# Phase rows and masks of small matrices moved from VectorE to GpSimd, and two weight loads joined

## The chip, the cores and the metric

The kernel runs on one core of one Trainium2 chip. The metric is the device time of one execution in microseconds (us); the median of several runs is compared. Beside the times there is one execution taken with a hardware profiler, from which all rows below come. The engines are named as in the profile: PE (matrix multiply), PEld (its weight loads), DVE (VectorE), ACT (ScalarE), POOL (GpSimd) and SP (SyncE, which here only issues DMAs).

## The reference

The input is one sequence of 2048 rows of 640 features in bfloat16. It is normalised, goes through a gated long convolution and through a dense two-layer network, and both results are joined:

```python
xn = _layernorm(x)                                  # x = A_q, 1 x 2048 x 640
k_shift = sum over t of k_pad[:, t:t+S, :] * shift_k[:, ks-1-t]      # ks = 4
kv = k_shift * v
y = irfft(rfft(kv padded to 2S) * rfft(ssm_k padded to 2S))[:S]      # float32, then bf16
s = xn * (y + kv * ssm_D)
g = silu(gelu(xn @ w1 + b1) @ w2 + b2)              # w1 640 x 1728, w2 1728 x 640
return x + s * g
```

## The kernel before

Partition p holds the 16 rows 16p to 16p+15 of the sequence. The 16 rows are worked in four chunks of four (`CH = 4`), so a chunk is 512 rows: it is normalised, transposed by PE into `xnT`, multiplied with w1 in 14 blocks of 128 columns (`ffn1`, L467, and `first_block`, L786, for the first six blocks of the first chunk), put through gelu by ACT into `hT`, and multiplied with w2 (L500).

The convolution is done as a Fourier transform of length 8192 in two factors. The first factor's matrices `WA` and `WB` are sines of integer phases: `prod` holds the phases (built at L304, cut to 13 bits by `f1_phase` at L308), and ACT takes the sines (`f1_sines`). The second factor uses three small 128x128 matrices `mats`, each made of 32x32 blocks on the diagonal. They too come from phases: `small_iotas` writes rows of column numbers with POOL (L340), `small_bits` takes bits of the partition number on DVE (a bitwise and at L350 and a cast at L352, for the masks 30, 1 and 96), `small_first` makes two scalars of them (L362, L363), `small_second` builds three phase rows `ph` (L356 twice, L371), `small_phase` finishes them, builds three masks (L377 to L381) and cuts the phases to five bits in `q` (L384, L385), ACT takes the sine (`small_sine`, L390), and DVE multiplies with the masks (`small_mats`, L394).

The order on each engine is written out by hand: first the function `prologue`, then a long list of steps, `PLAN`, each a short name that a table maps to a function. Each engine runs its own instructions in that order and waits only for what an instruction needs. So an engine that has little to do runs far ahead of the place in the program that the text suggests. In `PLAN`, `s` is `small_phase`, `w` is `f1_phase`, `X1` the load of the second chunk of x, `ls4` to `ls7` the second chunk's statistics (L421, L422), `lv1` its variance plus epsilon (L426), `lr1` the power to the -1/2 on POOL (L430), `lb1` the bias (L434), `ln4.d` to `ln7.a` its normalisation on DVE (L444) or ACT (L442), `tt` transposes on PE (L451), `cv` a step of the four-tap convolution on DVE (L590, L594, L583), `ss` and `sm` the sine and the product of the small matrices.

In `prologue` the first chunk is done by hand, in two halves of two rows: `bn` and `ag` are statistics (L748, L751), `sq` and `rc` the reciprocal root (L754 on ACT, L757 on DVE), `norm_dve` the normalisation (L760), `turn` the transposes on PE (L777), `turned_out` the copies back (L148 on DVE, L147 on ACT), and `first_block` the products with w1.

The loads are issued by SP (L239 for x, L266 for w1, L244 to L246 for k, L273 to L276 for w2, L269 for the filter, L249 for v), with four small ones on ACT's queue. Each load counts on one of eight semaphores in turn, and waits until the load eight places before it, on the same semaphore, has landed.

Of the kernel before, what the change touches and what calls it, by code (L numbers as in the profile page):

```python
# [15 lines left out]
ALU = mybir.AluOpType  # L16
# [4 lines left out]
F = 1728  # L21
# [11 lines left out]
TURNS = "231221331312001123202202330111320201303303312100"  # L33

PLAN = """
em6 he0 he1 s w X1 em7 em5 he2 K1 em4 ls6 ls7 ls4 ls5 K0 h11 he5 ee5.a ee4.a h8 h6 he4 ee7.a he3 he8 B1 h13 B2 B0 cv16
lv1 cv8 cv17 cv9 he6 lr1 lb1 C4 he13 ee6.a cv18 cv19 cv10 ln4.d h10 he11 he10 h7 he7 h12 h9 ln5.a he12 ln7.a ln6.d cv0
cv20 tt9 tt7 C1 C3 C0 he9 C2 cv11 cv1 te7.d cv21 ws0 tt6 tt8 te8.d g1 tt5 te9.d ss sm cv12 cv2 cv3 te5.d K3 X2 V5 K2
V4 V0 V3 V6 g0 ws1 ws2 ge0 ge1 g2 ge2 d kt1 kt7 kt6 kc7.a kt3 kt0 cv22 cv4 te6.d kc6.d kt2 kt9 kc3.d kc2.d kc0.a V2 X3
V7 kc9.d kc1.a kt12 kt4 kf2 kf23 kt11 kf8 ke2.d kc12.a V1 kt13 kc4.d kc13.d kf0 ke23.a ke8.a gm0.d kf6 kf22 ke6.a  # L40
# [51 lines left out]
def kernel(  # L92
# [15 lines left out]
    nc = tc.nc  # L108
# [127 lines left out]
    def load_x(c):  # L236
        for h in range(1 if c else 2):
            js = slice(2 * h, CH if c else 2 * h + 2)
            nc.sync.dma_start(out=xn_tiles[c][:, js, :], in_=x_v[:, c * CH:(c + 1) * CH, :][:, js, :])  # L239
# [22 lines left out]
                nc.scalar.dma_start(out=prm[FT:FT + DT, :], in_=A_ssm_D.rearrange("(t p) -> t p", p=P))  # L262

    def load_w1(i):
        a, b = ((0, 384), (384, 768), (768, F))[i]
        nc.sync.dma_start(out=w1_sb[:, :, a:b], in_=B_w1.rearrange("(t p) f -> p t f", p=P)[:, :, a:b])  # L266

    def load_kf(t):
# [63 lines left out]
    sm = {}  # L332
# [19 lines left out]
            nc.vector.tensor_copy(out=f, in_=i)  # L352
            sm.setdefault("in", []).append(f)

    def stt(o, a, s, b, op0, op1):
        nc.vector.scalar_tensor_tensor(out=o, in0=a, scalar=s, in1=b, op0=op0, op1=op1)  # L356

    def small_first():
        n_in, c_in, r_in = sm["in"]
        n_out, c_out, r_out = sm["cols"]  # L360
        sm.update(ph=scratch([3, P], F32), mask=scratch([3, P], F32), c8=scratch([1], F32), c16=scratch([1], F32))
        nc.vector.tensor_single_scalar(out=sm["c8"], in_=c_in, scalar=8.0, op=ALU.mult)  # L362
        nc.vector.tensor_single_scalar(out=sm["c16"], in_=c_in, scalar=16.0, op=ALU.mult)  # L363

    def small_second():
        n_in, c_in, r_in = sm["in"]
        n_out, c_out, r_out = sm["cols"]
        ph = sm["ph"]
        stt(ph[:, 0, :], n_out, n_in[:, 0:1], c_out, ALU.mult, ALU.add)
        stt(ph[:, 2, :], n_out, n_in[:, 0:1], c_out, ALU.mult, ALU.subtract)  # L370
        nc.vector.tensor_scalar(out=ph[:, 1, :], in0=ph[:, 2, :], scalar1=sm["c16"][:, 0:1], scalar2=None, op0=ALU.add)  # L371

    def small_phase():
        n_in, c_in, r_in = sm["in"]
        n_out, c_out, r_out = sm["cols"]
        ph, mask = sm["ph"], sm["mask"]
        nc.vector.tensor_scalar(out=ph[:, 2, :], in0=ph[:, 2, :], scalar1=8.0, scalar2=None, op0=ALU.add)  # L377
        nc.vector.tensor_scalar(out=ph[:, 0, :], in0=ph[:, 0, :], scalar1=sm["c8"][:, 0:1], scalar2=None, op0=ALU.subtract)
        nc.vector.tensor_scalar(out=mask[:, 0, :], in0=r_out, scalar1=r_in[:, 0:1], scalar2=None, op0=ALU.is_equal)
        for i in (1, 2):  # L380
            nc.vector.tensor_scalar(out=mask[:, i, :], in0=r_out, scalar1=r_in[:, 0:1], scalar2=2.0 / 4096.0,  # L381
                                    op0=ALU.is_equal, op1=ALU.mult)
        q = scratch([3, P], I32)
        nc.vector.tensor_single_scalar(out=q, in_=ph, scalar=float(8 + 16 + 128), op=ALU.add)  # L384
        nc.vector.tensor_single_scalar(out=q, in_=q, scalar=31, op=ALU.bitwise_and)  # L385
        sm.update(q=q, sn=scratch([3, P], F32))

# [352 lines left out]
    def prologue():  # L740
# [48 lines left out]
        make_identity(nc, ident[:])  # L789
        nc.vector.memset(prm[:], 0.0)  # L790
        load_x(0)
        for i in range(3):
# [118 lines left out]
```

## Time and profile before

| | before |
|---|---|
| median of 3 runs | 198.41 us (198.15 to 198.58) |
| the profiled execution's own time | 198.26 us |
| its span, first to last instruction | 196.5 us |
| PE busy | 186.5 us (95%) |
| DVE busy | 175.3 us (89%) |
| ACT busy | 162.6 us (83%) |
| POOL busy | 42.9 us (22%) |
| granted TensorE clock | 0.998 |

A row of the order of time gives the start in us, the time in us, the engine, the source line, the operation, what it writes and reads, the size, how many instructions are merged in the row, and in brackets the idle time before it with what ended it. A row of the table of waits gives who waited for whom, the total in us, how often, and the longest. A row of a table by stretch gives for each engine the busy time and, as (x), the instructions; then the clock, the DMA engines' share and GB/s.

### The profile page before, as it was taken

The numbers are of one execution on the slowest core, as the hardware profiler recorded it, in microseconds if no ns is written. First come the engines' busy times: TensorE is split into PE (matmuls) and PEld (weight loads), VectorE is DVE, ScalarE is ACT, GpSimd is POOL, SyncE is SP. The second block draws the span as 40 slices with busy tenths as digits, with TensorE's granted clock in tenths as the row PEclk, the third lists the DMA queues.
The fourth block names the chain that finished last, engine by engine and source line by source line (L and its number), as shares of the span: only waits on it lengthen the run. The fifth ranks groups of instructions, "written<-read, shape, count | busy, mean of one in ns | idle before, by whom it ended". The sixth has DMA issues, their size and how long they took to land.

```text
span 196.5 us, 5128 instructions
## 1 busy us (share of the span) xinstructions
PE 186.5 (95%) x1927; PEld 111.1 (57%) x1939; DVE 175.3 (89%) x379; ACT 162.6 (83%) x323; POOL 42.9 (22%) x76
## 2 busy tenths in 40 slices
PE   7899969999999999998999999999999999999991
PEld 2585447787665445663566443465665544657771
DVE  7989999999999999989999999999999920489992
ACT  3577999999999999999998999999679758991030
POOL 8100300004454032344030000000475500002220
PEclk9999999999999999999999999999999999999999
DMA  6999999974888899798788999596969659994344
GB/s 200 374 378 345 342 408 414 393 294 153 319 326 337 268 325 368 303 341 341 267 274 312 287 338 329 158 303 228 272 243 336 223 188 350 397 398 157 145 173 137
DMA packets 27057, 57.69 MB, mean 294 GB/s; under 512 B 3032, under 2 KB 15513, under 8 KB 27032
## 3 DMA queue, kind: packets, MB, share of 16 engines
q1 hardware_dynamic: 22528, 39.65, 57.6%
q0 software_dynamic: 4320, 17.70, 24.3%
q8 instruction: 15, 0.25, 0.5%
q14 instruction: 10, 0.08, 0.2%
q10 hardware_dynamic: 184, 0.01, 0.1%
HBM read 33.76 MB, written 18.35 MB: 265 GB/s over the span
## 4 chain that ended last, share of the span: by engine, by line
PE 59%; ACT 14%; DMA 12%; DVE 9%; issue 3%; SPq 1%; DVEq 0%
PE banks L500 20%; PE banks L467 19%; ACT area L147 7%; PE banks L414 7%; DMA area<-in_A_k_dram 5%; DMA area<-in_A_ssm_k_dram 5%; PE banks L550 5%; DVE area L590 3%; DMA w_sb<-in_B_w_dram 2%; ACT hT L479 2%; DVE area L594 2%; PE banks L719 2%; PE banks L720 2%; DVE area L148 2%; PE banks L451 1%
## 5 line engine op out<-in xcount | busy, mean ns | idle before, releaser
L147 ACT CAST area<-banks 128x426 bf16<-128x426 f32 (+2 forms) x175 | 80.7, 614 | 4.2 <-PE banks L414 3.4
L500 PE MATMUL banks<-w_sb,hT 128*128 128x320 bf16 (+1 forms) x462 | 65.8, 295 | 0.4 <-ACT sl L508 0.3
L500 PEld LDWEIGHTS <-hT 128*128 128x128 bf16 x462 | 43.5, 98 | 18.9 <-issue 3.7
L467 PE MATMUL banks<-xnT,w_sb 128*128 128x512 bf16 x218 | 52.8, 379 | 0.7
L674 DVE TENSOR_TENSOR area<-banks,area 128x426 bf16<-128x426 f32 (+1 forms) x96 | 50.1, 591 | 0.2
L479 ACT ACTIVATE hT<-banks,b_f 128x512 bf16<-128x512 f32 x52 | 35.4, 718 | 4.9 <-PE banks L467 3.0
L467 PEld LDWEIGHTS <-w_sb 128*128 128x128 bf16 x230 | 21.5, 97 | 25.7 <-issue 3.7
L508 ACT ACTIVATE sl<-banks 128x320 bf16<-128x320 f32 (+1 forms) x33 | 14.8, 476 | 14.2 <-PE banks L500 12.9
L594 DVE TENSOR_TENSOR area<-area 128x1280 bf16<-128x1280 bf16 x32 | 25.4, 816 | 0.3
L414 PE MATMUL banks<-area,mats 32*32 32x426 bf16 (+1 forms) x768 | 20.7, 345 | 0.5 <-DVE area L148 0.2
L728 DVE TENSOR_TENSOR area<-banks,xn 128x426 bf16<-128x426 f32 (+1 forms) x18 | 9.9, 591 | 12.3 <-ACT hT L479 10.2
L704 POOL DMA_DIRECT2D scrC<-area x16 | 11.7, 730 | 42.1 <-ACT area L147 40.0
L590 DVE TENSOR_TENSOR area<-area 128x1280 bf16<-128x1280 bf16 x24 | 19.1, 812 | 0.0
L550 PE MATMUL banks<-area,WA 128*128 128x212 bf16 (+1 forms) x64 | 15.6, 299 | 0.1
L550 PE MATMUL banks<-area,WB 128*128 128x214 bf16 (+1 forms) x64 | 15.5, 299 | 0.0
L565 POOL DMA_DIRECT2D scrK<-area x16 | 8.8, 553 | 29.3 <-ACT area L147 28.9
L414 PEld LDWEIGHTS <-mats 32*32 32x32 bf16 x768 | 8.1, 88 | 12.4 <-issue 10.3
L148 DVE CAST area<-banks 128x426 bf16<-128x426 f32 (+1 forms) x21 | 11.4, 593 | 1.6 <-PE banks L414 0.8
L576 POOL DMA_DIRECT2D scrU<-area x16 | 8.6, 543 | 14.5 <-ACT area L147 13.7
L430 POOL TENSOR_TENSOR rs<-ve,mhalf 128x4 f32<-128x4 f32 x3 | 4.0, 1350 | 31.0 <-DVE ve L426 31.0
L421 DVE BATCH_NORM_STATS2 st<-xn 128x6 f32<-128x320 bf16 x24 | 10.3, 472 | 0.0
L515 DVE TENSOR_TENSOR xn<-xn,sl 128x320 bf16<-128x320 bf16 (+1 forms) x33 | 9.8, 307 | 0.2 <-ACT sl L508 0.2
(106 smaller groups left out, 195.8 us busy)
## 6 DMA issues: line engine op xcount, KB each, us to landing
scrK<-area POOLq DMA_DIRECT2D x16, 320.0 KB, 3.2
scrU<-area POOLq DMA_DIRECT2D x16, 320.0 KB, 3.7
area<-scrK SPq DMA_DIRECT2D x16, 320.0 KB, 6.6
area<-area SPq DMA_DIRECT2D x32, 160.0 KB, 3.8
area<-scrU SPq DMA_DIRECT2D x16, 320.0 KB, 4.8
scrC<-area POOLq DMA_DIRECT2D x16, 320.0 KB, 4.2
area<-scrC SPq DMA_DIRECT2D x16, 320.0 KB, 6.5
area<-in_A_k_dram SPq DMA_DIRECT2D x4, 640.0 KB, 10.0
```

Source lines behind the costliest of these rows:

```text
L147: return nc.scalar.copy(out=out_ap, in_=in_ap)
L148: return nc.vector.tensor_copy(out=out_ap, in_=in_ap)
L414: nc.tensor.matmul(out=out[b, :], lhsT=mats[a, m, a], rhs=rhs[a, :], start=start, stop=stop)
L467: nc.tensor.matmul(out=ps, lhsT=w1_sb[:, t, ft * P:(ft + 1) * P], rhs=xnT[:, t, :], start=(t == 0), stop=(t == DT - 1))
L479: nc.scalar.activation(out=hT[:, ft, :], in_=one(("h", i)), func=ACT.Gelu_apprx_tanh, bias=b1_f[:, ft:ft + 1], scale=1.0)
L500: nc.tensor.matmul(out=ps[:, 0:ws.stop - ws.start], lhsT=hT[0:M, ft, q * P:(q + 1) * P], rhs=w2_sb[0:M, ft, hs.start + ws.start:hs.start + ...
L508: nc.scalar.activation(out=sl[:, ws], in_=one(key)[:, 0:ws.stop - ws.start], func=ACT.Silu)
L550: nc.tensor.matmul(out=ps[:, dst], lhsT=(WA, WB)[r][:, n2, :], rhs=rows[:, n2 % 2, src], start=True, stop=True)
L590: nc.vector.tensor_tensor(out=uc, in0=uc, in1=tmp, op=ALU.add)
L594: nc.vector.tensor_tensor(out=tmp if s else uc, in0=kh[:, r0:r0 + KC, :], in1=w_exp[:, j:j + 1, :].to_broadcast([P, KC, D]), op=ALU.mult)
L674: nc.vector.tensor_tensor(out=flat(("p", i))[:, x * w:x * w + w], in0=one(("mu", i))[:, 0:w], in1=flat(key)[:, cols(j)], op=ALU.mult)
L704: nc.gpsimd.dma_start(out=pair_view(scrC)[g2], in_=pair(("c", g2)))
```

## The change

Three things are changed.

The three phase rows, their two additions and the three masks are built by POOL instead of DVE. The two instructions that DVE did with two operands and a scalar (L356) become one product and two additions of two operands, so POOL has nine instructions for DVE's eight. They are all in `small_second` now.

The two bit steps that stay on DVE (`small_phase`) move in `PLAN` from in front of `w` to behind `lv1`.

The first two loads of w1, columns 0 to 383 and 384 to 767, become one. Eight loads then come before the second chunk's x instead of nine.

```diff
 PLAN = """
-em6 he0 he1 s w X1 em7 em5 he2 K1 em4 ls6 ls7 ls4 ls5 K0 h11 he5 ee5.a ee4.a h8 h6 he4 ee7.a he3 he8 B1 h13 B2 B0 cv16
-lv1 cv8 cv17 cv9 he6 lr1 lb1 C4 he13 ee6.a cv18 cv19 cv10 ln4.d h10 he11 he10 h7 he7 h12 h9 ln5.a he12 ln7.a ln6.d cv0
+em6 he0 he1 w X1 em7 em5 he2 K1 em4 ls6 ls7 ls4 ls5 K0 h11 he5 ee5.a ee4.a h8 h6 he4 ee7.a he3 he8 B1 h13 B2 B0 cv16
+lv1 s cv8 cv17 cv9 he6 lr1 lb1 C4 he13 ee6.a cv18 cv19 cv10 ln4.d h10 he11 he10 h7 he7 h12 h9 ln5.a he12 ln7.a ln6.d
...
     def load_w1(i):
-        a, b = ((0, 384), (384, 768), (768, F))[i]
+        a, b = ((0, 768), (768, F))[i]
...
     def small_second():
...
-        stt(ph[:, 0, :], n_out, n_in[:, 0:1], c_out, ALU.mult, ALU.add)
-        stt(ph[:, 2, :], n_out, n_in[:, 0:1], c_out, ALU.mult, ALU.subtract)
-        nc.vector.tensor_scalar(out=ph[:, 1, :], in0=ph[:, 2, :], scalar1=sm["c16"][:, 0:1], scalar2=None, op0=ALU.add)
+        nc.gpsimd.tensor_scalar(out=ph[:, 1, :], in0=n_out, scalar1=n_in[:, 0:1], scalar2=None, op0=ALU.mult)
+        nc.gpsimd.tensor_tensor(out=ph[:, 0, :], in0=ph[:, 1, :], in1=c_out, op=ALU.add)
+        nc.gpsimd.tensor_tensor(out=ph[:, 2, :], in0=ph[:, 1, :], in1=c_out, op=ALU.subtract)
+        nc.gpsimd.tensor_scalar(out=ph[:, 1, :], in0=ph[:, 2, :], scalar1=sm["c16"][:, 0:1], scalar2=None, op0=ALU.add)
+
+        mask = sm["mask"]
+        nc.gpsimd.tensor_scalar(out=ph[:, 2, :], in0=ph[:, 2, :], scalar1=8.0, scalar2=None, op0=ALU.add)
+        nc.gpsimd.tensor_scalar(out=ph[:, 0, :], in0=ph[:, 0, :], scalar1=sm["c8"][:, 0:1], scalar2=None, op0=ALU.subtract)
+        nc.gpsimd.tensor_scalar(out=mask[:, 0, :], in0=r_out, scalar1=r_in[:, 0:1], scalar2=None, op0=ALU.is_equal)
+        for i in (1, 2):
+            nc.gpsimd.tensor_scalar(out=mask[:, i, :], in0=r_out, scalar1=r_in[:, 0:1], scalar2=2.0 / 4096.0,
+                                    op0=ALU.is_equal, op1=ALU.mult)

     def small_phase():
-        nc.vector.tensor_scalar(out=ph[:, 2, :], in0=ph[:, 2, :], scalar1=8.0, scalar2=None, op0=ALU.add)
-        nc.vector.tensor_scalar(out=ph[:, 0, :], in0=ph[:, 0, :], scalar1=sm["c8"][:, 0:1], scalar2=None, op0=ALU.subtract)
-        nc.vector.tensor_scalar(out=mask[:, 0, :], in0=r_out, scalar1=r_in[:, 0:1], scalar2=None, op0=ALU.is_equal)
-        for i in (1, 2):
-            nc.vector.tensor_scalar(out=mask[:, i, :], in0=r_out, scalar1=r_in[:, 0:1], scalar2=2.0 / 4096.0,
-                                    op0=ALU.is_equal, op1=ALU.mult)
         q = scratch([3, P], I32)
-        nc.vector.tensor_single_scalar(out=q, in_=ph, scalar=float(8 + 16 + 128), op=ALU.add)
+        nc.vector.tensor_single_scalar(out=q, in_=sm["ph"], scalar=float(8 + 16 + 128), op=ALU.add)
         nc.vector.tensor_single_scalar(out=q, in_=q, scalar=31, op=ALU.bitwise_and)
```

POOL's queue of the kernel after the change, from the two memsets of the prologue to the power of the second chunk (`rs`; `area` holds the phase rows and masks). Before, L430 followed the memsets directly:

```order
13 L803 MEMSET hT 1x512
14 L804 MEMSET area 1x1920
15 L366 TENSOR_SCALAR area<-area 128x128
16 L367 TENSOR_TENSOR area<-area 128x128
17 L368 TENSOR_TENSOR area<-area 128x128
18 L369 TENSOR_SCALAR area<-area 128x128
19 L372 TENSOR_SCALAR area<-area 128x128
20 L373 TENSOR_SCALAR area<-area 128x128
21 L374 TENSOR_SCALAR area<-area 128x128
22 L376 TENSOR_SCALAR area<-area 128x128 x2
23 L427 TENSOR_TENSOR rs_360<-ve_352,mhalf 128x4
```

Nine instructions now stand between the memsets and the power. The first of them waits for the cast of the mask 30 (L352) on DVE; the fourth waits for the scalar that DVE makes at L363 before the change (L360 after it).

DVE's queue before the change, from the copies of the bias and D (`b_f`, `dD_sb`) to the first statistics of the second chunk (`st`; the 128x2048 row is `f1_phase`):

```order
31 L854 CAST b_f<-banks 128x14
32 L855 COPY dD_sb<-banks 128x5
33 L356 SCALAR_TENSOR_TENSOR area<-area 128x128 x2
34 L371 TENSOR_SCALAR area<-area 128x128
35 L377 TENSOR_SCALAR area<-area 128x128
36 L378 TENSOR_SCALAR area<-area 128x128
37 L379 TENSOR_SCALAR area<-area 128x128
38 L381 TENSOR_SCALAR area<-area 128x128 x2
39 L384 TENSOR_SCALAR area<-area 128x384
40 L385 TENSOR_SCALAR area<-area 128x384
41 L308 TENSOR_SCALAR area<-area 128x2048
42 L421 BN_STATS st_299<-xn 128x6 x2
```

The same queue after the change, in two pieces: behind the copies, and around `ve`, the variance plus epsilon of the second chunk.

```order
31 L851 CAST b_f<-banks 128x14
32 L852 COPY dD_sb<-banks 128x5
33 L308 TENSOR_SCALAR area<-area 128x2048
34 L418 BN_STATS st_297<-xn 128x6 x2
...
42 L591 TENSOR_TENSOR area<-area 128x1280
43 L423 TENSOR_SCALAR ve_352<-mv_298 128x4
44 L381 TENSOR_SCALAR area<-area 128x384
45 L382 TENSOR_SCALAR area<-area 128x384
46 L591 TENSOR_TENSOR area<-area 128x1280 x3
```

The eight rows of 128x128 are gone from DVE, and the two of 128x384 (L384 and L385 before, L381 and L382 after) now stand behind `ve`. All other instructions of DVE, and all of PE and ACT, keep their order.

More of the change, by code (lines that the diff above doesn't have):

```diff
@@ L35 @@
 PLAN = """
-em6 he0 he1 s w X1 em7 em5 he2 K1 em4 ls6 ls7 ls4 ls5 K0 h11 he5 ee5.a ee4.a h8 h6 he4 ee7.a he3 he8 B1 h13 B2 B0 cv16
-lv1 cv8 cv17 cv9 he6 lr1 lb1 C4 he13 ee6.a cv18 cv19 cv10 ln4.d h10 he11 he10 h7 he7 h12 h9 ln5.a he12 ln7.a ln6.d cv0
-cv20 tt9 tt7 C1 C3 C0 he9 C2 cv11 cv1 te7.d cv21 ws0 tt6 tt8 te8.d g1 tt5 te9.d ss sm cv12 cv2 cv3 te5.d K3 X2 V5 K2
-V4 V0 V3 V6 g0 ws1 ws2 ge0 ge1 g2 ge2 d kt1 kt7 kt6 kc7.a kt3 kt0 cv22 cv4 te6.d kc6.d kt2 kt9 kc3.d kc2.d kc0.a V2 X3
-V7 kc9.d kc1.a kt12 kt4 kf2 kf23 kt11 kf8 ke2.d kc12.a V1 kt13 kc4.d kc13.d kf0 ke23.a ke8.a gm0.d kf6 kf22 ke6.a
+em6 he0 he1 w X1 em7 em5 he2 K1 em4 ls6 ls7 ls4 ls5 K0 h11 he5 ee5.a ee4.a h8 h6 he4 ee7.a he3 he8 B1 h13 B2 B0 cv16
+lv1 s cv8 cv17 cv9 he6 lr1 lb1 C4 he13 ee6.a cv18 cv19 cv10 ln4.d h10 he11 he10 h7 he7 h12 h9 ln5.a he12 ln7.a ln6.d
+cv0 cv20 tt9 tt7 C1 C3 C0 he9 C2 cv11 cv1 te7.d cv21 ws0 tt6 tt8 te8.d g1 tt5 te9.d ss sm cv12 cv2 cv3 te5.d K3 X2 V5
+K2 V4 V0 V3 V6 g0 ws1 ws2 ge0 ge1 g2 ge2 d kt1 kt7 kt6 kc7.a kt3 kt0 cv22 cv4 te6.d kc6.d kt2 kt9 kc3.d kc2.d kc0.a V2
+X3 V7 kc9.d kc1.a kt12 kt4 kf2 kf23 kt11 kf8 ke2.d kc12.a V1 kt13 kc4.d kc13.d kf0 ke23.a ke8.a gm0.d kf6 kf22 ke6.a
 ke22.a kt5 kf10 kf38 kc11.d ke0.d kt8 kf4 kc8.d kc5.d ke10.a ke38.a kf9 kt10 ke9.a ke4.a kt15 kc15.d kc10.d kt14 kf1
@@ L353, in small_bits @@
             sm.setdefault("in", []).append(f)
-    def stt(o, a, s, b, op0, op1):
-        nc.vector.scalar_tensor_tensor(out=o, in0=a, scalar=s, in1=b, op0=op0, op1=op1)
     def small_first():
@@ L368, in small_second @@
         ph = sm["ph"]
-        stt(ph[:, 0, :], n_out, n_in[:, 0:1], c_out, ALU.mult, ALU.add)
-        stt(ph[:, 2, :], n_out, n_in[:, 0:1], c_out, ALU.mult, ALU.subtract)
-        nc.vector.tensor_scalar(out=ph[:, 1, :], in0=ph[:, 2, :], scalar1=sm["c16"][:, 0:1], scalar2=None, op0=ALU.add)
-    def small_phase():
-        n_in, c_in, r_in = sm["in"]
-        n_out, c_out, r_out = sm["cols"]
-        ph, mask = sm["ph"], sm["mask"]
-        nc.vector.tensor_scalar(out=ph[:, 2, :], in0=ph[:, 2, :], scalar1=8.0, scalar2=None, op0=ALU.add)
-        nc.vector.tensor_scalar(out=ph[:, 0, :], in0=ph[:, 0, :], scalar1=sm["c8"][:, 0:1], scalar2=None, op0=ALU.subtract)
-        nc.vector.tensor_scalar(out=mask[:, 0, :], in0=r_out, scalar1=r_in[:, 0:1], scalar2=None, op0=ALU.is_equal)
-        for i in (1, 2):
-            nc.vector.tensor_scalar(out=mask[:, i, :], in0=r_out, scalar1=r_in[:, 0:1], scalar2=2.0 / 4096.0,
-                                    op0=ALU.is_equal, op1=ALU.mult)
+        nc.gpsimd.tensor_scalar(out=ph[:, 1, :], in0=n_out, scalar1=n_in[:, 0:1], scalar2=None, op0=ALU.mult)
[9 more added lines that the diff above has]
+                                    op0=ALU.is_equal, op1=ALU.mult)
+    def small_phase():
         q = scratch([3, P], I32)
-        nc.vector.tensor_single_scalar(out=q, in_=ph, scalar=float(8 + 16 + 128), op=ALU.add)
+        nc.vector.tensor_single_scalar(out=q, in_=sm["ph"], scalar=float(8 + 16 + 128), op=ALU.add)
         nc.vector.tensor_single_scalar(out=q, in_=q, scalar=31, op=ALU.bitwise_and)
@@ L791, in prologue @@
         load_x(0)
-        for i in range(3):
+        for i in range(2):
             load_w1(i)
```

## The prediction

> **What bounds the kernel now.** I read the busy time by stretch first, then the table of waits, then the order of time around the lines that the diff touches. The first view has, per stretch, the busy time of PE, PEld, DVE, ACT and POOL.
>
> ```profile
> core 0: us, PE busy (x) PEld busy (x) DVE busy (x) ACT busy (x) POOL busy (x), PEclk, DMA share, GB/s
> ...
> 8.48:20.00 11.52, 11.47 (x92) 8.20 (x94) 10.59 (x39) 8.96 (x17) 0.00 (x0) 1.00 1.04 367
> 20.00:100.00 80.00, 77.27 (x670) 48.17 (x674) 78.33 (x151) 79.46 (x164) 20.47 (x34) 1.00 0.88 324
> 100.00:180.00 80.00, 79.09 (x1034) 42.89 (x1041) 66.85 (x139) 68.53 (x132) 14.64 (x24) 1.00 0.82 283
> ```
>
> Three stretches, three limits. From 8.48 to 20 us PE is full (11.47 of 11.52) and ACT waits for it. From 20 to 100 us ACT is full: 79.46 of 80.00, so no more than 0.54 us can be won there unless ACT begins earlier or loses work, and the change takes nothing off ACT. From 100 us PE is full again. DVE, which the change relieves, is nearly full in the middle stretch (78.33) but is not the last to arrive, as the waits of the first 45 us say (who <- for whom: us in total, times, longest):
>
> ```profile
> PE banks L451 <- DVE xn L444: 1.5, 1, 1.5
> ...
> ACT hT L479 <- PE banks L786: 1.5, 2, 0.9
> ...
> ACT hT L479 <- PE banks L467: 0.4, 1, 0.4
> ...
> ACT area L147 <- PE banks L550: 0.2, 1, 0.2
> ```
>
> From 12 us on ACT's waits (1.5, 0.4, 0.2 us) are all for PE; none is for DVE. One wait on DVE's rows stands on PE, 1.5 us long, for the normalised rows of the second chunk (L444). Before 8.48 us a single chain sets PE's start:
>
> ```profile
> 6.03 0.15 DVE L352 CAST area<-area 128x1 f32<-128x1 int32 x1
> 6.39 0.17 DVE L757 RECIPROCAL rstd<-sd 128x2 f32<-128x2 f32 x1 [0.21 <-ACT sd L754]
> 6.60 0.80 DVE L760 TENSOR_SCALAR xn<-xn,mv,rstd 128x640 bf16<-128x640 bf16 x2
> ...
> 7.83 0.56 DVE L148 COPY xnT<-banks 128x768 bf16<-128x768 bf16 x1
> ...
> 7.10 0.81 PE L777 MATMUL banks<-ident,xn 128*128 128x128 bf16 x10 [0.77 <-DVE xn L760]
> 7.84 0.71 PE L645 MATMUL banks<-skT,ident 4*128 4x320 bf16 x4
> 8.48 0.28 PE L786 MATMUL banks<-xnT,w_sb 128*128 128x256 bf16 x1
> ```
>
> The two L760 normalise rows 0 and 1 of the first chunk; PE transposes them (L777), DVE copies them back (L148), and the first block of w1 (L786) starts. Whatever delays an L760 delays L786, and with it the full PE, then the full ACT, to the end.
>
> **The part on DVE.** These rows go or move:
>
> ```profile
> 11.62 0.14 DVE L363 TENSOR_SCALAR area<-area 128x1 f32<-128x1 f32 x1
> ...
> 12.87 0.60 DVE L356 SCALAR_TENSOR_TENSOR area<-area 128x128 f32<-128x128 f32 x2
> ...
> 14.76 0.35 DVE L384 TENSOR_SCALAR area<-area 128x384 int32<-128x384 f32 x1
> 15.15 0.36 DVE L385 TENSOR_SCALAR area<-area 128x384 int32<-128x384 int32 x1
> 15.42 1.22 DVE L308 TENSOR_SCALAR area<-area 128x2048 int32<-128x2048 int32 x1
> ...
> 21.27 0.16 DVE L426 TENSOR_SCALAR ve<-mv 128x4 f32<-128x4 f32 x1
> ```
>
> From 12.87 to 14.76 stand the eight instructions that leave DVE: 1.89 us. L384 and L385 (14.76 to 15.42, 0.66 us) move behind L426. So ve, and the rstd that hangs on it, come 2.55 us earlier, near 18.7. What that is worth is read where PE waited:
>
> ```profile
> 25.21 0.93 ACT L442 ACTIVATE xn<-xn,nb,rs 128x640 bf16<-128x640 bf16 x1
> ...
> 26.02 0.80 DVE L444 TENSOR_SCALAR xn<-xn,mv,rs 128x640 bf16<-128x640 bf16 x2
> ...
> 26.52 1.31 PE L451 MATMUL banks<-ident,xn 128*128 128x128 bf16 x16 [1.45 <-DVE xn L444]
> ...
> 30.04 0.60 ACT L390 ACTIVATE area<-area,sin_bias 128x384 f32<-128x384 int32 x1
> ...
> 31.41 0.54 DVE L394 TENSOR_TENSOR mats<-area 128x384 bf16<-128x384 f32 x1
> ```
>
> DVE's two rows now come near 24, but every transposed block needs all four rows of the chunk, and the last one is ACT's L442, done at 25.21 + 0.93 = 26.14. ACT's queue is full in front of it, so it does not move. PE's 16 transposes then end near 26.14 plus 13 or so of them, about 0.6 us earlier than now: PE's 1.45 us of waiting becomes about 0.85. The lead that PE and DVE have then meets the full ACT. DVE's own lead of about 1.9 us is cut too: the matrices (L394) wait for ACT's sine L390, done at 30.64, so that DVE stands there from about 29.5 and leaves with about 0.7 us in hand; behind it wait only copies and products that had come early. L385's result is needed at 30.04 and is there near 20. So the gain is what ACT's own waits give back: at least 0, at most 0.54 us. I take 0.2, the wait for L550 in the table.
>
> **The part on GpSimd.** Nine instructions of 128x128 f32 come in front of L430. The trace has few POOL instructions of that size; the nearest are these, with what DVE ran beside them:
>
> ```profile
> 21.59 1.48 POOL L430 TENSOR_TENSOR rs<-ve,mhalf 128x4 f32<-128x4 f32 x1 [15.72 <-DVE ve L426]
> ...
> 21.34 2.29 DVE L594 TENSOR_TENSOR area<-area 128x1280 bf16<-128x1280 bf16 x3
> ...
> L594 DVE TENSOR_TENSOR area<-area 128x1280 bf16<-128x1280 bf16 x32 | 25.4, 816 | 0.3
> ...
> 101.14 1.03 POOL L430 TENSOR_TENSOR rs<-ve,mhalf 128x4 f32<-128x4 f32 x1 [9.35 <-DVE ve L426]
> ...
> 100.93 3.15 DVE L674 TENSOR_TENSOR area<-banks,area 128x426 bf16<-128x426 f32 x6
> ...
> 102.26 0.24 POOL L614 IOTA kn<- 128x128 int16 x1
> 102.60 0.61 POOL L615 TENSOR_SCALAR kn<-kn,kcol 128x128 int16<-128x128 int16 x1
> ```
>
> One operand and 128x128 takes 0.61 us (L615). With two operands: not under 0.61, not over the 1.03 of L430's power; I take 0.70, near the one of its size. The second L430 ran beside L674, which has one operand in PSUM; the first ran beside L594, with both in SBUF, and took 0.45 longer. L594 goes at (2.29 - 0.82) / 2 = 0.74 us a piece, with 0.816 for one alone (its group), so the one that held the engine at 21.59 had until 22.08: 0.49 us, about the 0.45 that L430 lost. So whoever comes second waits for the other's instruction, and POOL gets in between two DVE instructions that stand back to back.
>
> Now the start. POOL's queue is empty after its memset:
>
> ```profile
> 4.17 1.69 POOL L807 MEMSET area<- 1x1920 bf16 x1
> ```
>
> It ends at 5.86, and the first of the nine needs only the first mask's cast, L352, done at 6.18. POOL began L430 0.16 us after L426's end (21.43 to 21.59); so it begins at 6.34 and lasts 0.61, to 6.95. That is across the first L760, due at 6.60. Three of the nine can run there; the fourth needs L363's result at 11.76.
>
> Cost if DVE waits: the first L760 starts at 6.95, 0.35 late. The second POOL instruction reads what the first wrote, is ready 0.10 later (L614's end at 102.50 to L615's start) at 7.05, and waits for the first L760; it then goes ahead of the second L760, which waits its 0.70. Together 0.35 + 0.70 = 1.05 us on the chain to L786. Cost if DVE does not wait: 0. If the third also gets ahead: 1.75. Below nothing it cannot be, since POOL takes no step off that chain. I take 1.05: the trace shows the later one waiting, and here POOL is first.
>
> The Trainium skill ("SBUF — State Buffer", Who interferes with whom) says that the two engines share one pair of ports as an exclusive lock, whoever starts first keeps it for its whole instruction, and that DVE needs it for a tensor_scalar in a two-port mode. By that rule both L760 wait and the sum is the forecast's; were it not so for DVE, the sum would be the first rival's. The L430 rows agree for POOL as the later one, and no row of this trace has DVE as the later one.
>
> The other six run from 11.8 + 1.05 on, 6 x 0.61 = 3.7 us, and meet L308 (1.22): done by about 18 at the latest, before the power's input at 18.7 + 1.05. So L430, which is next behind them in POOL's queue, is not held up. L308 may wait up to 0.61 for one of them; ACT reads its result only behind the L442 that ends at 26.14, so that costs nothing.
>
> **The part on SP.** w1's columns 0 to 767 come as one load.
>
> ```profile
> SPq L266 <- DMA skp<-in_A_shift_k_dram: 1.3, 1, 1.3
> ...
> 4.39 0.52 SPq L239 DMA_DIRECT2D xn<-in_A_q_dram  x1
> ...
> w_sb<-in_B_w_dram SPq DMA_DIRECT2D x3, 480.0 KB, 5.6
> ...
> 1.64 4.56 DMA w_sb<-in_B_w_dram
> ```
>
> The first 480 KB landed at 6.20; at the 367 GB/s of the stretch behind, the other 491,520 bytes take 1.34 us, so the merged load lands near 7.5, 0.9 us before L786 needs it. Loads behind it wait, each for the one eight places ahead, as before; the 1.3 us that the third load of w1 stood for skp now falls on the second chunk's x, which stood until 4.39 anyway. The engines move 1.04 of their share either way: 0.
>
> **Sum.** The profiled execution took 198.26 us, its span 196.5. 198.26 + 1.05 - 0.20 = 199.11. The median of the runs was 0.15 above the profiled one: 199.26, rounded to 199.2.
>
> **Rivals.** A difference under 0.2%, 0.4 us, cannot be told from none here.
>
> - DVE does not wait, or loses to POOL nowhere on the chain: 198.41 - 0.20 = 198.2, between 197.9 and 198.4. For it: no row shows DVE held up by POOL. Against: L430's 0.45. Chance 0.22, of which 0.07 faster.
> - One collision only: DVE keeps its place for the second L760. 198.41 + 0.35 - 0.20 = 198.6. Chance 0.20, 0.17 of it no change.
> - Faster: DVE's earlier rows are worth what PE waited for them. If L442 and the ACT in front of it have slack that the busy view hides, PE's wait goes by 0.6 to 1.45 us, and 197.0 to 197.8 follows. It decides only if ACT's 79.46 of 80 is not real work. Chance 0.08.
> - Three collisions: 198.41 + 1.75 - 0.20 = 200.0. Chance 0.10.
> - The merged load lands behind 8.48: every us late is a us; 0.9 us of margin speak against it. 198.8 if 0.4 late. Chance 0.03.
>
> The forecast has 0.37. Faster 0.07 + 0.08 = 0.15; no change 0.15 + 0.17 = 0.32; slower 0.37 + 0.10 + 0.03 + 0.03 = 0.53. The range, 198.0 to 199.8, leaves out the faster rival and the three collisions, and takes in a two-operand instruction of up to 1.0 us plus part of the doubt on ACT.
>
> **What would show it.** In the profile after: three POOL rows from about 6.3 us; the first L760's successor starting near 6.95 instead of 6.60, the second some 0.7 behind that; L786 first at 9.5 and ACT's first L479 as much later. ve near 18.7 plus that delay; PE's wait at L451 down from 1.45 to about 0.85; a new wait of about 1 us of DVE for ACT ahead of the matrices; ACT still full from 21 to 100 us. Wrong if L786 starts at 8.5 (then DVE did not wait) or if PE's wait at L451 is gone and ACT's later rows come earlier by as much (then ACT was not the limit).

## The result: 0.64 us faster, and where the time came from

| | before | after |
|---|---|---|
| median, 13 runs of each | 198.41 us (198.15 to 199.36) | 197.77 us (197.64 to 198.32) |
| the profiled execution's own time, its span | 198.26 us, 196.5 us | 197.71 us, 195.9 us |

The ratio is 0.9974, with a 95% interval of 0.9967 to 0.9982: faster by a quarter of a per cent, where 199.2 us was forecast, in a range from 198.0 to 199.8, and slower thought the likeliest. Lines behind the edited functions now have numbers three lower: L757 is the old L760, L783 the old L786, L439 and L441 the old L442 and L444, L448 the old L451, L547 the old L550.

First the start of the changed kernel, in order of time, POOL and DVE and PE:

```profile
6.39 0.61 POOL L366 TENSOR_SCALAR area<-area 128x128 f32<-128x128 f32 x1 [0.51 <-DVE area L352]
7.08 0.41 POOL L367 TENSOR_TENSOR area<-area 128x128 f32<-128x128 f32 x1
7.45 0.49 POOL L368 TENSOR_TENSOR area<-area 128x128 f32<-128x128 f32 x1
...
6.62 1.05 DVE L757 TENSOR_SCALAR xn<-xn,mv,rstd 128x640 bf16<-128x640 bf16 x2
7.59 0.48 DVE L745 BATCH_NORM_STATS2 stats<-xn 128x6 f32<-128x320 bf16 x1
...
8.76 0.61 PE L783 MATMUL banks<-xnT,w_sb 128*128 128x256 bf16 x4
```

The three POOL rows stand where they were forecast, across the first two normalisations. But the first of these starts at 6.62 beside POOL's row, not behind it, and the pair takes 1.05 us in place of 0.80. The first block of w1 starts at 8.76 in place of 8.48: 0.28 us lost, not 1.05.

Then the second chunk, ACT, DVE and PE:

```profile
18.98 0.16 DVE L423 TENSOR_SCALAR ve<-mv 128x4 f32<-128x4 f32 x1
...
24.41 0.80 DVE L441 TENSOR_SCALAR xn<-xn,mv,rs 128x640 bf16<-128x640 bf16 x2
...
25.50 0.93 ACT L439 ACTIVATE xn<-xn,nb,rs 128x640 bf16<-128x640 bf16 x1
...
26.48 0.90 PE L448 MATMUL banks<-ident,xn 128*128 128x128 bf16 x13 [0.97 <-ACT xn L439]
...
30.95 0.56 DVE L391 TENSOR_TENSOR mats<-area 128x384 bf16<-128x384 f32 x1 [1.07 <-ACT area L387]
```

This went as forecast: ve at 18.98, DVE's rows 1.6 us earlier, PE's wait cut from 1.45 to 0.97 and now ended by ACT's row, and DVE waiting 1.07 us for the sine. What PE won shows at ACT, at 38 us. Before, then after, in order of time:

```profile
37.78 1.17 ACT L147 CAST area<-banks 128x426 bf16<-128x426 f32 x2
39.10 2.61 ACT L147 CAST area<-banks 128x428 bf16<-128x428 f32 x6 [0.16 <-PE banks L550]
41.62 0.69 ACT L147 COPY area<-banks 128x640 bf16<-128x640 bf16 x1
```

```profile
38.03 3.51 ACT L147 CAST area<-banks 128x426 bf16<-128x426 f32 x8
41.28 0.85 ACT L147 COPY area<-banks 128x640 bf16<-128x640 bf16 x1
```

The eight CASTs are the same. Before, they take 3.93 us from the first start to the last end (37.78 to 41.71), with two waits for PE's L550 among them; after, 3.51 us with none. The COPY behind them ended at 42.31 and now ends at 42.13, although ACT came to the CASTs 0.28 us (0.25 by the rows) later: 0.46 us won, on an engine that is full.

Last the end, in the table of waits of SP over the last 5 us, before and after:

```profile
SPq L906 <- DMA out_dram<-xn: 1.5, 1, 1.5
SPq L906 <- PEq L906: 0.7, 2, 0.5
```

```profile
SPq L903 <- DMA out_dram<-xn: 1.0, 2, 0.8
SPq L903 <- PEq L903: 0.6, 2, 0.5
```

Behind the last store SP waits for all loads and stores to be done, one semaphore after another in a fixed order, about 0.06 us each. The records of these waits in the trace give:

| us | last store issued | its landing seen | last of these waits | end of span |
|---|---|---|---|---|
| before | 193.28 | 195.16 (second wait of nine) | 195.59 | 196.48 |
| after | 193.16 | 195.01 (the last wait) | 195.01 | 195.90 |

The loads and stores take the eight semaphores in turn. With one load fewer the last store falls on another one, which happens to be the last that is waited for: the 0.43 us of waits that stood behind its landing are now over before it lands.

So, against the profiled execution: 198.26 + 0.28 (start) - 0.46 (ACT at 38 us) + 0.06 (given back in small steps from 50 to 130 us) - 0.43 (end) = 197.71. Of the 0.89 us won, 0.43 come from a count of loads, which no step of the prediction had, and 0.26 of the rest from two waits that it priced too low.

### The profile page after: what moved, and what is told of

It is laid out like the page before. It is cut to its first block, busy times and chain, and to the rows that moved or that the text cites. A ratio compares the mean times of both kernels' runs of the same rounds, so it can differ in the third digit from the quotient of the medians.

```text
span 195.9 us, 5143 instructions
## 1 busy us (share of the span) xinstructions
PE 187.5 (96%) x1939; PEld 111.3 (57%) x1939; DVE 174.0 (89%) x371; ACT 162.6 (83%) x323; POOL 49.0 (25%) x85
## 4 chain that ended last, share of the span: by engine, by line
PE 71%; ACT 18%; DVE 7%; issue 3%; POOL 0%; POOLq 0%; ACTq 0%; DVEq 0%
PE banks L497 23%; PE banks L464 21%; ACT area L147 8%; PE banks L411 7%; PE banks L547 5%; ACT hT L476 4%; PE banks L783 3%; PE banks L536 2%; PE banks L716 2%; PE banks L448 2%; ACT sl L505 2%; PE banks L717 2%; DVE area L587 2%; DVE area L304 1%; PE banks L460 1%
## 5 line engine op out<-in xcount | busy, mean ns | idle before, releaser
L464 PE MATMUL banks<-xnT,w_sb 128*128 128x512 bf16 x230 | 53.6, 379 | 0.1
L547 PE MATMUL banks<-area,WA 128*128 128x212 bf16 (+1 forms) x64 | 15.6, 299 | 0.0
L547 PE MATMUL banks<-area,WB 128*128 128x214 bf16 (+1 forms) x64 | 15.3, 299 | 0.0
L734 POOL DMA_DIRECT2D out_dram<-area x6 | 3.3, 549 | 29.4 <-DVE area L730 21.9
```

The lines of the kernel that those rows point to most:

```text
L464: nc.tensor.matmul(out=ps, lhsT=w1_sb[:, t, ft * P:(ft + 1) * P], rhs=xnT[:, t, :], start=(t == 0), stop=(t == DT - 1))
L547: nc.tensor.matmul(out=ps[:, dst], lhsT=(WA, WB)[r][:, n2, :], rhs=rows[:, n2 % 2, src], start=True, stop=True)
```

## The experiments

At first theory A says just this sum, and theory B says that the gain is DVE's relief, or a better start by the joined load, and the end an accident of one execution; later runs state theories of their own, each in its expectation. For each kernel that was run the table gives, from its profiled execution, how much later than in the kernel before ACT's row near 14 us starts, with the parts of that (x's load landing later; POOL beside the first two normalisations; PE waiting for w1), what changed at 38 to 41 us, what was given back behind that up to the last product, and the time from the landing of the last store to the last wait. All in us, worked out from the starts and ends of the same instructions in the traces; "joined" marks the joined load. The part of x comes and goes from one execution to the next, whatever the kernel, and medians under some 0.3 us apart have to be read with that. A ratio is not the quotient of the two medians: where the times of a kernel spread widely, it can lie up to 0.0015 from it.

| kernel | start: x + POOL + w1 | at 38 us | behind | last waits | span |
|---|---|---|---|---|---|
| before | 0 | 0 | 0 | 0.43 | 196.48 |
| after (POOL, joined) | 0.02 + 0.26 + 0 | -0.46 | +0.06 | 0 | 195.90 |
| joined load alone | 0.06 + 0 + 0.35 | 0 | +0.04 | 0 | 196.40 |
| POOL move alone | 0.30 + 0.26 + 0 | -0.46 | +0.06 | 0.43 | 196.81 |
| masks first (POOL, joined) | 0.11 + 0 + 0.03 | -0.46 | +0.45 | 0 | 196.36 |
| two bit steps only (joined) | 0.20 + 0 + 0, other 0.18 | 0 | 0 | 0 | 196.28 |
| after, last store back | 0 + 0.26 + 0 | -0.46 | 0 | 0.43 | 196.11 |
| before, last store moved | 0.09 + 0 + 0 | 0 | +0.06 | 0 | 196.22 |
| masks alone | 0.38 + 0 + 0 | -0.45 | +0.05 | 0.43 | 196.29 |
| masks, last store moved | 0.01 + 0 + 0 | -0.28 | +0.06 | 0 | 195.96 |
| wide first POOL row (joined) | 0.15 + 0.40 + 0 | -0.46 | +0.06 | 0 | 196.13 |
| POOL move, three loads, same end | 0.12 + 0.26 + 0 | -0.46 | +0.06 | 0 | 196.17 |
| all POOL rows late, three loads | 0.05 + 0 + 0 | -0.46 | +0.05 | 0 | 195.68 |
| after, again (POOL, joined) | 0.03 + 0.26 + 0.66 | -0.46 | +0.05 | 0 | 196.55 |

The "other 0.18" is PE's: its last seven warm-up products L767 took up to 0.63 us each in that execution, where 0.38 is usual, and the transposes stood behind them. What the columns leave, up to 0.2 us, is the time from the last store's issue to its landing, 1.70 to 2.06 us from one execution to the next.

### The two halves of the change

The joined load alone:

```diff
-        a, b = ((0, 384), (384, 768), (768, F))[i]
+        a, b = ((0, 768), (768, F))[i]
...
-        for i in range(3):
+        for i in range(2):
             load_w1(i)
```

> The kernel before with one edit: w1's first two loads as one. Theory A (the gain of 0.64 us sits mostly behind the last store: with one load fewer the last store moves to the semaphore that is waited for last, 0.44 us): about 197.95 us, ratio 0.9977; the first block of w1 starts at 8.5 us as in the kernel before, ACT's waits at 38 to 39 us are still there, and the end of the span comes 0.07 us behind the last store's landing instead of 0.5. Theory B (the gain comes from DVE's relief): 198.4, ratio 1.000.

Measured: 198.15 us, ratio 0.9986 (0.9977 to 0.9996). The gain at the end is there and ACT's waits at 38 us are too, as A has it; the interval leaves out B's 1.000. But the first block is not at 8.5:

```profile
8.31 0.29 PE L645 MATMUL banks<-skT,ident 4*128 4x320 bf16 x1
8.89 0.83 PE L786 MATMUL banks<-xnT,w_sb 128*128 128x256 bf16 x6 [0.28 <-DVE stats L748]
```

PE stands 0.28 us before it. DVE's copy of the transposed rows had ended at 8.45; what came last was the joined load, which took 7.2 us from issue to landing here, and 5.7 in the profiled execution of the changed kernel. The row names statistics of DVE, on which these products do not depend; the second run of the changed kernel, below, names the load.

The move to POOL alone, with w1 in three loads:

```diff
-        a, b = ((0, 768), (768, F))[i]
+        a, b = ((0, 384), (384, 768), (768, F))[i]
```

> The changed kernel with w1 in three loads again. Theory A: about 198.3 us, ratio 0.9995: the first block at 8.76, ACT's waits for L550 at 38 to 39 us gone, ACT's row at 41 us about 0.2 to 0.3 us earlier than before, and the old 0.5 us behind the last store. Theory B: about 197.8, ratio 0.997.

Measured: 197.99 us, ratio 0.9993 (0.9981 to 1.0004). The table shows A's parts one by one: 0.26 lost at the start, 0.46 won at 38 us, the old 0.43 at the end. The interval of the ratio excludes B's 0.997 and holds A's 0.9995. The median alone would not decide: seven of the eleven times lie from 197.85 to 198.19 us and four from 198.59 to 198.82, and 197.99 is nearer to B's 197.8 than to A's 198.3.

### What the start costs

```diff
     def small_second():
+        mask = sm["mask"]
+        nc.gpsimd.tensor_scalar(out=mask[:, 0, :], in0=r_out, scalar1=r_in[:, 0:1], scalar2=None, op0=ALU.is_equal)
+        for i in (1, 2):
+            nc.gpsimd.tensor_scalar(out=mask[:, i, :], in0=r_out, scalar1=r_in[:, 0:1], scalar2=2.0 / 4096.0,
+                                    op0=ALU.is_equal, op1=ALU.mult)
         nc.gpsimd.tensor_scalar(out=ph[:, 1, :], in0=n_out, scalar1=n_in[:, 0:1], scalar2=None, op0=ALU.mult)
```

> The changed kernel with GpSimd's three mask rows ahead of the phase rows; they wait for a cast of DVE at about 11.5 us, so that no GpSimd instruction runs beside the first two normalisations. Theory A (the two normalisations lost 0.12 and 0.14 us to GpSimd, and this start is lost up to the end): first block back at 8.5 us, total down by up to 0.28 us from the changed kernel, to about 197.5. Rival: the start is absorbed by ACT's queue: first block at 8.5, total the same 197.8. If the normalisations still take 0.56 us, GpSimd was not what they lost to.

Measured: 197.64 us, ratio 0.9969 (0.9957 to 0.9981). In order of time, with no POOL row before 11.9 us:

```profile
6.71 0.80 DVE L757 TENSOR_SCALAR xn<-xn,mv,rstd 128x640 bf16<-128x640 bf16 x2
...
8.62 1.16 PE L783 MATMUL banks<-xnT,w_sb 128*128 128x256 bf16 x9
```

The pair is back at 0.80 us, so POOL was what it lost to. That the start is kept to the end is seen best in the run that has it without the joined load (the last but one, below). In this profiled execution 0.39 us were lost again at 110 us, where DVE waited 0.46 us for a load of the convolution; no other profiled execution shows that.

How DVE loses was asked with a first POOL row of three times the width:

```diff
-        nc.gpsimd.tensor_scalar(out=ph[:, 1, :], in0=n_out, scalar1=n_in[:, 0:1], scalar2=None, op0=ALU.mult)
+        nc.gpsimd.tensor_scalar(out=ph, in0=n_out[:, None, :].to_broadcast([P, 3, P]), scalar1=n_in[:, 0:1], scalar2=None, op0=ALU.mult)
```

> The changed kernel with GpSimd's first row three times as wide (128x384 in place of 128x128, the same products written to all three phase rows), so that it lies across both first normalisations. If DVE loses a share of its speed while GpSimd runs beside it, each normalisation again takes 0.56 to 0.57 us and the first block starts at 8.76 us, give or take the x load. If DVE waits for a GpSimd instruction it meets, the first normalisation ends behind the wide one, near 8 us, and the first block starts near 9.6 us. If the loss is per GpSimd instruction, the first normalisation loses 0.12 us and the second nothing: 8.6 us.

```profile
6.52 1.25 POOL L366 TENSOR_SCALAR area<-area 128x384 f32<-128x384 f32 x1 [0.64 <-DVE area L352]
...
6.75 1.20 DVE L757 TENSOR_SCALAR xn<-xn,mv,rstd 128x640 bf16<-128x640 bf16 x2
...
9.04 0.72 PE L783 MATMUL banks<-xnT,w_sb 128*128 128x256 bf16 x5
```

Measured: 197.91 us in the one run. POOL runs from 6.52 to 7.77, and DVE starts inside that and ends at 7.95: it does not stand behind POOL. The pair loses 0.40 us (1.20 against 0.80) in about 1.1 us of POOL beside it, and lost 0.25 in about 1.0 us in the changed kernel. It is not a wait for a whole instruction (9.6 us was expected for that) and not a sum per POOL instruction (8.6). As a share of the time that POOL runs beside, it is a quarter in one kernel and over a third in the other, and it is not even: by their records, the two normalisations took 0.52 and 0.76 us, not 0.56 and 0.57. Counted by the columns that POOL finished while the pair ran, it is 1.0 ns each in both (0.25 for two rows of 128, 0.40 for one of 384). So DVE may be slowed, or held for a part of each POOL row; two executions do not tell these apart.

Nor is it always DVE that loses. Two kernels below have POOL's masks beside DVE's two L356. The rows, POOL then DVE, first of the masks alone, then of the masks with the last store moved:

```profile
12.83 1.53 POOL L381 TENSOR_SCALAR area<-area 128x128 f32<-128x128 f32 x2
...
13.25 0.61 DVE L356 SCALAR_TENSOR_TENSOR area<-area 128x128 f32<-128x128 f32 x2
```

```profile
12.46 1.41 POOL L381 TENSOR_SCALAR area<-area 128x128 f32<-128x128 f32 x2
...
12.88 0.79 DVE L356 SCALAR_TENSOR_TENSOR area<-area 128x128 f32<-128x128 f32 x2
```

The order is the same, but in the first POOL loses 0.12 us and DVE nothing (0.60 before), in the second DVE loses 0.19 and POOL nothing. What decides who loses was not found.

Beside a long row of DVE, POOL does wait. Rows of POOL and DVE, in order of time, first from the changed kernel's profile, where POOL's L372 meets DVE's L308, then from its second profiled execution (the last run below), where L372 is through before L308 begins and L373 meets it:

```profile
12.92 1.59 POOL L372 TENSOR_SCALAR area<-area 128x128 f32<-128x128 f32 x1
14.58 0.61 POOL L373 TENSOR_SCALAR area<-area 128x128 f32<-128x128 f32 x1
...
13.14 1.22 DVE L308 TENSOR_SCALAR area<-area 128x2048 int32<-128x2048 int32 x1
```

```profile
12.93 0.53 POOL L372 TENSOR_SCALAR area<-area 128x128 f32<-128x128 f32 x1
13.54 1.64 POOL L373 TENSOR_SCALAR area<-area 128x128 f32<-128x128 f32 x1
```

L308 takes the same 1.22 us as in the kernel before, and L372 loses 1.06 (1.59 against 0.53), in the other execution L373 as much (1.64 against 0.61). L308 does not always go free: where POOL's masks came first ("masks first" and "all POOL rows late"), it took 1.34 and 1.38 us. The Trainium skill ("SBUF — State Buffer", Who interferes with whom) has one rule for both engines, for DVE in a two-port mode: whoever issues first holds the shared ports for its whole instruction, and the other "**fully blocks** (not throttle)". That POOL stands still agrees with the second half of it, but by the records L372 had begun 0.22 us ahead of L308 and lost all the same (the profile calls POOL's spans rough, so who was first there stays open). The wide row fits it neither way by the records: were POOL first, the first normalisation could not have ended inside the row (at 7.27, the row at 7.77); were DVE first, the second would have had to wait for the row's end, and it ended only 0.18 us behind it, where the two start 0.36 us apart without POOL. Unless POOL holds the ports for less than its record shows, the measurement decides against the rule here.

### What DVE's relief is worth

Only the two bit steps moved, all rows still on DVE, with the joined load:

```diff
-em6 he0 he1 s w X1 em7 em5 he2 K1 em4 ls6 ls7 ls4 ls5 K0 h11 he5 ee5.a ee4.a h8 h6 he4 ee7.a he3 he8 B1 h13 B2 B0 cv16
-lv1 cv8 cv17 cv9 he6 lr1 lb1 C4 he13 ee6.a cv18 cv19 cv10 ln4.d h10 he11 he10 h7 he7 h12 h9 ln5.a he12 ln7.a ln6.d cv0
+em6 he0 he1 w X1 em7 em5 he2 K1 em4 ls6 ls7 ls4 ls5 K0 h11 he5 ee5.a ee4.a h8 h6 he4 ee7.a he3 he8 B1 h13 B2 B0 cv16
+lv1 s cv8 cv17 cv9 he6 lr1 lb1 C4 he13 ee6.a cv18 cv19 cv10 ln4.d h10 he11 he10 h7 he7 h12 h9 ln5.a he12 ln7.a ln6.d cv0
```

> The kernel before with the joined load, and of the move only the two bit steps (0.66 us of DVE) behind the second chunk's statistics; phase rows and masks stay on DVE, and GpSimd gets nothing. Theory A (ACT's two waits at 38 to 39 us go as soon as DVE is a little earlier; no loss at the start): 197.5 us, ratio 0.9955. Theory B (what counts is how much leaves DVE): 0.66 of 2.55 us, so a quarter of the gain, 197.9 with the joined load.

Measured: 197.94 us, ratio 0.9993 (0.9977 to 1.0009), with the joined load's end in it. A's time was wrong; the median fits B, but not by B's reason, since none of the middle's gain is there (and the interval takes in 1.000 as well). In order of time, DVE, PE and ACT (lines one lower than before):

```profile
20.98 0.16 DVE L425 TENSOR_SCALAR ve<-mv 128x4 f32<-128x4 f32 x1
...
26.39 0.80 DVE L443 TENSOR_SCALAR xn<-xn,mv,rs 128x640 bf16<-128x640 bf16 x2
...
26.89 1.31 PE L450 MATMUL banks<-ident,xn 128*128 128x128 bf16 x16 [1.45 <-DVE xn L443]
...
39.47 2.61 ACT L147 CAST area<-banks 128x428 bf16<-128x428 f32 x6 [0.15 <-PE banks L549]
```

ve comes earlier, but the normalisations come 0.37 us later than before, just as the whole execution does. They stand behind the two bit steps in DVE's queue either way: work that is moved from one place ahead of them to another place ahead of them is no relief. What counts for PE is the work in front of L443, not the time of ve.

The three masks alone on POOL, with the rest as before:

```diff
-        nc.vector.tensor_scalar(out=mask[:, 0, :], in0=r_out, scalar1=r_in[:, 0:1], scalar2=None, op0=ALU.is_equal)
+        nc.gpsimd.tensor_scalar(out=mask[:, 0, :], in0=r_out, scalar1=r_in[:, 0:1], scalar2=None, op0=ALU.is_equal)
         for i in (1, 2):
-            nc.vector.tensor_scalar(out=mask[:, i, :], in0=r_out, scalar1=r_in[:, 0:1], scalar2=2.0 / 4096.0,
+            nc.gpsimd.tensor_scalar(out=mask[:, i, :], in0=r_out, scalar1=r_in[:, 0:1], scalar2=2.0 / 4096.0,
```

> The kernel before with only the three mask rows on GpSimd (0.7 us less on DVE ahead of the second chunk's normalisation, against 1.9 in the changed kernel, and GpSimd idle until 11.5 us). Theory A (PE's transposes of the second chunk are held by DVE only up to where ACT's own row ends, 0.4 us earlier; from there more relief is worth nothing): PE's wait at its transposes ends with ACT's row, ACT's two waits for L550 at 38 to 39 us go, 0.46 us less after 41 us: about 197.9 us. Rival (the gain grows with the work taken off DVE): a third of it, 198.2.

Measured: 197.99 us, ratio 0.9972 (0.9962 to 0.9983), A's time. DVE, PE and ACT:

```profile
25.95 0.80 DVE L444 TENSOR_SCALAR xn<-xn,mv,rs 128x640 bf16<-128x640 bf16 x2
...
26.45 1.31 PE L451 MATMUL banks<-ident,xn 128*128 128x128 bf16 x16 [1.00 <-DVE xn L444]
...
38.14 3.50 ACT L147 CAST area<-banks 128x426 bf16<-128x426 f32 x8
```

This execution runs 0.38 us late, so DVE's rows are 0.45 us earlier against the rest (26.02 + 0.38 - 25.95), PE's wait is 0.45 shorter, and ACT wins 0.45 with its waits gone. The whole 0.46 is to be had with a quarter of the relief. But the reason that A gave is not what the row shows: PE's wait is still ended by DVE. The cap is not where PE meets ACT's row at 26 us, but where ACT's two waits at 38 us are used up.

### The end

One spare load more, issued by SP ahead of the first late load of q:

```diff
+    spare = consts.tile([P, 8, 4], BF16, name="spare")
...
+        if i == 0:
+            nc.sync.dma_start(out=spare[:, i, :], in_=A_shift_k[0:P, :])
```

> The changed kernel with one spare load of 128x4 (into a tile that nothing reads), issued ahead of the first of the eight late loads of q, so that the number of loads on the sync queue is that of the kernel before and the last store falls on its old semaphore. Theory A (0.43 us of the gain is the order in which the last waits stand): everything up to the last store as in the changed kernel, landing to last wait back from 0.06 to 0.43 us, total up by 0.4 to about 198.2. Rival (the end has nothing to do with it): 197.8.

b2's load, which is issued by GpSimd in place of SP:

```diff
-            nc.sync.dma_start(out=w2_sb[FLAST:FLAST + 1, FT - 1, :], in_=B_b2.rearrange("(o d) -> o d", o=1))
+            nc.gpsimd.dma_start(out=w2_sb[FLAST:FLAST + 1, FT - 1, :], in_=B_b2.rearrange("(o d) -> o d", o=1))
```

> The kernel before, with only the load of b2 (1.2 KB) issued by GpSimd instead of the sync engine: one load fewer on the sync queue, w1 in its three loads, nothing moved from DVE. Theory A: the last store falls on the semaphore that is waited for last, total down by 0.4 us to about 198.0, first block at 8.5 us. Rival (the joined load of w1 gains by itself, by a lighter queue at the start): 198.4.

Measured: 198.12 us, ratio 0.9984 (0.9974 to 0.9994), for the spare load in the changed kernel, and 197.98 us, ratio 0.9974 (0.9963 to 0.9985), for b2's load in the kernel before. The first gives back 0.35 of 0.64 us by the medians of two different sets of runs, and 0.2 us by the ratios; the intervals of the two ratios (0.9984 here, 0.9974 for the changed kernel) overlap, so alone it would not settle it. The second does: a kernel that leaves POOL's rows, the loads of w1 and the middle as they were (the table has 0 at 38 us) is as fast against the kernel before as the changed kernel is. Its waits of SP at the end:

```profile
SPq L906 <- DMA out_dram<-xn: 0.9, 1, 0.9
```

### Versions that put it together

The masks on POOL and b2's load on GpSimd:

> The kernel before with the three mask rows on GpSimd and b2's load issued by GpSimd: both gains without the collision at the first normalisations and without the longer first load. Theory A: -0.46 - 0.43, about 197.5 us, under the changed kernel's 197.8. Rival: one of the two is worth nothing, 197.9 to 198.0.

Measured: 197.77 us, ratio 0.9967 (0.9955 to 0.9979): 0.27 us short of A. The end is there in full, the middle with 0.28 only:

```profile
25.76 0.80 DVE L444 TENSOR_SCALAR xn<-xn,mv,rs 128x640 bf16<-128x640 bf16 x2
...
37.77 3.68 ACT L147 CAST area<-banks 128x426 bf16<-128x426 f32 x8
```

The L356 pair took 0.60 us before and takes 0.79 here beside POOL's masks (0.61 in the masks alone, as shown above), so that DVE's normalisations come 0.27 us earlier, not 0.45, and ACT wins 0.28 and keeps part of a wait (3.68 us for its eight rows against 3.50). With the masks alone (0.45 for 0.45) and the changed kernel (0.46 for 1.9) this fits one reading: ACT wins what DVE's rows win, one for one, up to 0.46.

The changed kernel with three loads of w1 and b2 on GpSimd, so that only the join is undone; the same with the masks first, so that no POOL row runs before 11.5 us; and the changed kernel beside them:

> The changed kernel with w1 in three loads again and b2's load issued by GpSimd, so that the number of loads on the sync queue, and the place of the last store in the last waits, are those of the changed kernel: only the joined load is undone. Theory A (the joined load gains only by the end, and by itself is late in some executions): the same as the changed kernel or up to 0.2 us faster, 197.6 to 197.8. Rival (the joined load also gains at the start): 198.2.

> The run before this one with GpSimd's three mask rows ahead of its phase rows, so that all nine start behind 11.5 us: the full relief of DVE (-0.46 at 38 to 39 us), the end (-0.43), no collision at the first normalisations and no joined load. Theory A: first block at 8.5 us, 197.5 us. Rival (relief given back elsewhere): 197.8.

> The changed kernel again, beside the three others on one chip: 197.8 us, ratio 0.9974.

Measured: 197.89 us, ratio 0.9975 (0.9964 to 0.9985); 197.50 us, ratio 0.9958 (0.9946 to 0.9970); and 197.86 us, ratio 0.9977 (0.9965 to 0.9988). The joined load is worth nothing but its count: without it, the same time. What it risks is seen in the third:

```profile
9.43 0.28 PE L783 MATMUL banks<-xnT,w_sb 128*128 128x256 bf16 x1 [0.59 <-DMA w_sb<-in_B_w_dram]
```

PE stood 0.59 us for it, from 8.84 to 9.43. Of seven profiled executions with the joined load two show such a wait (0.28 and 0.59 us); of the seven with three loads none does. The second of the three has the lowest median, 0.4% under the kernel before and 0.36 us under the changed one, at the 197.5 us that the sum gave: 198.41 - 0.46 - 0.43 = 197.5. Its interval still touches the changed kernel's (0.9970 against 0.9965), and with parts of up to 0.3 us that come and go, a hit to the tenth is partly luck. Its ACT and PE rows:

```profile
8.53 1.16 PE L783 MATMUL banks<-xnT,w_sb 128*128 128x256 bf16 x9
...
37.80 3.50 ACT L147 CAST area<-banks 128x426 bf16<-128x426 f32 x8
```

## Why the prediction was wrong

**The collision at the start: right place, wrong size.** POOL's first row came at 6.39 (6.34 forecast) and lasted 0.61, three rows ran there. "Cost if DVE waits", 0.35 + 0.70 = 1.05 us, was taken for the forecast; it measured 0.26. The step that failed is "whoever comes second waits for the other's instruction": it was read off POOL's L430, as the later one, and carried over to DVE as the later one, which no row of the trace showed. DVE lost 0.12 and 0.14 us on the two normalisations and was not held to the end of POOL's instruction. The bound "not under 0.61" for the two-operand rows was wrong as well: they took 0.41 and 0.49 us, less than the one with a scalar from a column.

**The middle: right mechanism, wrong size.** ve, PE's new wait (0.97 against 0.85), its new end in ACT's row and DVE's wait for the sine (1.07 against 1) came as forecast. But of the gain 0.20 was taken, "the wait for L550 in the table", and it measured 0.46. The idle time that a view gives is not what a wait costs. The ends of the CASTs are 0.42 us apart when nothing is waited for, while one that has waited lasts 0.51 to 0.52; before, two of the ends were 0.63 and 0.67 apart, 0.46 us lost in two gaps of 0.11 and 0.16. A row that has waited also loses its overlap with the row before it, about 0.10 us each time. So that the gain stayed under 0.54, the bound read from ACT's idle time, is luck: only 0.27 us of it were idle, the other 0.19 stood in the busy time as lost overlap, and a bound on idle time does not cap that. The Trainium skill ("Perfetto Trace Analysis", Optimizing Scalar/DVE Operations) gives a ground on which one could have known: the latency that a profile shows is about twice an instruction's overhead of reaching its data, since the half in which the write is acknowledged lies beside the next instruction. The trace agrees in that these rows overlap, by 0.10 to 0.16 us before the change.

**The end: not in the sum.** "The engines move 1.04 of their share either way: 0" was said of the joined load, and worked out for the start only. That SP waits for eight semaphores in a row at the end, and that a load fewer moves the last store among them, was the largest single step but one, 0.43 us, and it needed no trace of the changed kernel: the order of the waits and the count of the loads stand in the kernel before.

**The joined load: right in the execution that was profiled, too sure beyond it.** It landed near 7.4 us, 7.5 forecast. But its landing differs by 2 us between executions (5.7 to 7.7 us from issue), against a margin of 0.9, so the rival with a chance of 0.03 came true in two of seven profiled executions.

**The rivals.** "DVE does not wait", 198.2 us, was the nearest by its mechanism. That "no row shows DVE held up by POOL" was written down against the forecast, but the cases were none, one, two or three whole instructions, and a part of one was not among them. The faster rival's span, 197.0 to 197.8, takes in the 197.77, but by luck: it had neither the loss at the start nor the gain at the end, and took what PE's wait loses, 0.6 us or more, for the whole gain. Its condition, that ACT's busy time is not all real work, held for 0.19 us. (The sum itself, 199.26, rounds to 199.3 and not to 199.2; nothing hangs on it.)

## What to carry to other kernels

Count the loads and stores: where the end of a kernel waits for its DMA semaphores one by one, the last store should be on the one that is waited for last, and an edit that adds or takes away a load anywhere turns that wheel. Price a wait on a full engine by the distance of the ends around it, against the distance of the same rows undisturbed, and not by the idle time shown; and price relief by what stands in front of the late row in its queue, since a step moved to another place ahead of it gives nothing. A row on a neighbour engine that slowed the first chain cost to the end here, so give such a row something late to wait for.

## What was not expected of the hardware

- DVE's two normalisations beside POOL lost 0.25 us in 1.0 us (128x128 rows) and 0.40 in 1.1 us (mostly one 128x384 row), while POOL beside DVE's L308 lost 1.06 in 1.22 us. Beside the same masks, DVE's L356 lost 0.19 us in one execution and nothing in another, where POOL lost 0.12.
- On POOL a 128x128 row with a scalar from a column took 0.61 us, and one with two operands of that size 0.41 us; 128x384 with the scalar took 1.25 us, two of the small ones.
- Each wait for DMA semaphores at the end took about 0.06 us even if it was met long before, and the last store, of 128x160, took 1.70 to 2.06 us from issue to landing.
